# Query weights ahead of the first keys on the load queue, and one half of the key transpose further back, in a decode attention kernel

## The chip, the core and the metric

The kernel runs on one core of a Trainium2 chip. The metric is the device time of one execution in microseconds (us). Engines are called by short names: PE is the matrix engine (TensorE), PEld its weight loads, DVE the vector engine, ACT the scalar engine, POOL the GpSimd engine and SP the engine that issues most transfers. The 16 DMA engines bring data from the device memory (HBM) into the on-chip memory.

## What is computed

Eight sequences, one new token each. The token vectors (8 x 512) are normalized, an attention over the last 1024 cached positions gives s, a feed-forward network gives a gate g, and the output is x + s * g.

```python
xn = _layernorm(x)
q  = xn @ wq                            # 32 query heads of 128, 8 key/value heads
k  = k_cache[:, :, Sk - W:, :]          # W = 1024 of 4096 positions
v  = v_cache[:, :, Sk - W:, :]
p  = softmax(q . k * Dh ** -0.5)
s  = (p . v) @ wo                       # 4096 -> 512
g  = silu((gelu(xn @ w_gate) * (xn @ w_up)) @ w_down)
out = x + s * g
```

wq and wo have 4 MB each, the three feed-forward weights 1.75 MB each, and the windows of K and V 2 MB each for every one of the 8 batches. All of it is bf16 and is read once.

## The kernel before

**Loads.** The large arrays go through a pool of eight slots of 2 MB (`slot`, L62). `load_cache` (L70) loads K or V of one batch into a slot by two transfers of 1 MB, one for each group `g` of four heads; a partition receives one contiguous row of 8 KB. wq fills two slots, by two transfers of 2 MB with rows of 16 KB (L90 to L95). All of these are issued by SP, in the order of the program: `load_k(0)`, wq, `load_k(1)`, `load_v(0)`, and then, in the loop over batches (L399), `load_k(b + 2)` and `load_v(b + 1)`; behind the loop the feed-forward weights and wo (L420 to L438), the last quarter of wo in three pieces. A tile that needs a slot takes the one that has been out of use longest, and SP then also waits for the engine that read it last. A transfer also waits for the one that used the same completion semaphore before: there are eight of these, shared in turn by SP's transfers and the four small ones of x, which ACT issues (L68).

**Front.** DVE computes the statistics of x (L129) and the normalized x, PE transposes it, and DVE writes `xnR` (L153). Between them DVE, POOL and ACT prepare constants (L170 to L224). Then 32 matmuls (L248) multiply `xnR` with wq into eight accumulators, ACT and DVE cast them to bf16 (L258), DVE transposes them in 32 x 32 blocks (L261), and 16 copies by DVE and ACT (L270) place them in `qbd`, the block-diagonal query. `qbd` was set to zero before (L240).

**Batches.** K comes with positions on the partitions. `turn_k(b, g)` (L233) transposes one half of K of a batch on DVE, in 32 x 32 blocks of pairs, into one of three buffers `kT`. `scores(b, g)` (L281) multiplies with `qbd` on PE, eight matmuls for each half. `softmax(b)` (L304) takes the maximum on DVE and the exponential on ACT, `turn_p` (L327) transposes the probabilities on DVE, and `values(b)` (L334) multiplies with V on PE. `gather` and `regroup` (L355, L373) collect heads after batches 4 and 7. The schedule is written out by hand: each engine does its instructions in the order of the program. Before the loop, DVE has

```python
    turn_k(0, 0)
    turn_k(0, 1)
    nc.vector.memset(qbd, 0.0)
```

and then the casts, transposes and copies for q. In the loop the order for batch b is `turn_k(b+1, 0)`, `softmax(b)`, `scores(b+1, 0)`, `turn_k(b+1, 1)`, `scores(b+1, 1)`, `turn_p(b)`, `values(b)`.

**End.** The feed-forward network (L444 to L492) and the product with wo (L496 to L505, 32 matmuls for each of four quarters of wo) follow, then the gate and the residual (L507, L509) and the store (L511).

Of the kernel before, what the change touches and what calls it, by code (L numbers as in the profile page):

```python
# [21 lines left out]
def kernel(  # L22
# [13 lines left out]
    nc = tc.nc  # L36
# [25 lines left out]
    def slot(name):  # L62
        return ring.tile([P, 2 * ROW], BF16, name=name, tag="slot")
# [6 lines left out]
    def load_cache(cache, b, name):  # L70
        t = slot(name).rearrange("p (g x) -> p g x", g=NG)
        for g in range(NG):
            nc.sync.dma_start(  # L73
                out=t[:, g],
                in_=cache[b, g * HG : (g + 1) * HG, win0:Sk, :].rearrange(
                    "n (p c) d -> p n (c d)", c=C
                ),
            )
        return t
# [3 lines left out]
    def load_k(b):  # L83
        k_sb[b] = load_cache(A_k_cache, b, "k_sb")

    def load_v(b):
        v_sb[b] = load_cache(A_v_cache, b, "v_sb")

    load_k(0)
    wq_v = A_wq.rearrange("(p k) n -> p k n", k=NK)  # L90
    wq_sb = []
    for i in range(2):
        t = slot("wq_sb").rearrange("p (k n) -> p k n", k=NK // 2)
        nc.sync.dma_start(out=t, in_=wq_v[:, i * (NK // 2) : (i + 1) * (NK // 2), :])  # L94
        wq_sb += [t[:, k, :] for k in range(NK // 2)]  # L95
    load_k(1)
    load_v(0)

# [130 lines left out]
    qbd = keep.tile([P, 2, B, 2, NG, 4 * Hq], BF16, name="qbd")  # L229
# [3 lines left out]
    def turn_k(b, g):  # L233
        t = kT_pool.tile([P, ROW], BF16, name="kT")
        nc.vector.transpose(out=t.bitcast(I32), in_=k_sb[b][:, g].bitcast(I32))  # L235
        kT[b, g] = t

    turn_k(0, 0)
    turn_k(0, 1)
    nc.vector.memset(qbd, 0.0)  # L240
    q_both = slot("q_both")
    q_bf = q_both[:, 0:ROW]
    q_t = q_both[:, ROW : 2 * ROW]
# [20 lines left out]
    for j in range(4):  # L264
        sl = slice(32 * j, 32 * j + 32)
        for m in range(2):
            for g in range(NG):
                e = nc.scalar.copy if (4 * j + 2 * m + g) % 3 == 2 else nc.vector.tensor_copy
                c0 = j * Hq + g * qd
                e(out=qbd[sl, m, :, :, g, c0 : c0 + qd], in_=q_v[sl, m, :, 0, :, g, :])  # L270


    pT, S, P_sb, O_ps = {}, {}, {}, {}
# [270 lines left out]
```

## Time and profile before

| what | value |
|---|---|
| median of 3 runs | 121.66 us (121.61 to 121.68) |
| the profiled execution's own time | 121.48 us |
| its span in the profile | 119.4 us |
| busy in the span: DVE, PE, ACT, POOL | 75.8, 73.0, 31.4, 3.2 us |
| read from HBM | 47.46 MB, 397 GB/s over the span |
| K and V transfers: issue to landing, median | 19.7 and 20.0 us |

The span is the time between the first and the last record of the profiled execution; 2.1 us lie around it. A line of a timeline gives the start and the busy time in us, the engine, the line of the kernel, the operation, what it writes and reads, and in brackets how long the engine had been idle before it and what ended that wait. In the row of 40 slices each digit is the busy share in tenths, so a slice is 2.985 us.

### The profile page before, as it was taken

Reading aid. Unit: us, or ns where it says so; the run is one execution under the profiler, and the core shown is the slowest. Engines: PE = TensorE matmul, PEld = TensorE weight load, DVE = VectorE, ACT = ScalarE, POOL = GpSimd, SP = SyncE. Lnnn points to the kernel's source line nnn. Section 1 sums busy time; section 2 is a strip of 40 time slices with the busy share of each in tenths; the row PEclk is TensorE's granted clock in tenths of the full one; section 3 lists DMA queues with packets and bytes.
Section 4 is the critical chain, followed back from the end, with each engine's and each line's share of the span. In section 5 each row is a group of like instructions: output and inputs, shape, how many; then the busy total and the mean of one; then the engine's idle time right before and its main releaser. Section 6 shows DMA issues by size and latency. Waiting matters only on the chain.

```text
span 119.4 us, 2300 instructions
## 1 busy us (share of the span) xinstructions
PE 73.0 (61%) x985; PEld 38.7 (32%) x992; DVE 75.8 (63%) x101; ACT 31.4 (26%) x75; POOL 3.2 (3%) x10
## 2 busy tenths in 40 slices
PE   0001499811994987969687674991994547545370
PEld 0000134300341544535443351450453433143350
DVE  1048978399739999999959959909943241651000
ACT  2233000676007052341712510700616211200000
POOL 2006100000000000000000000000000000000000
PEclk9999999985599999999999998599589855555555
DMA  1999999999999999999999999999999999999930
GB/s 47 411 445 417 434 425 431 417 428 434 428 420 425 431 423 423 428 423 431 417 431 420 431 423 423 428 428 423 420 434 439 437 433 418 427 421 417 412 148 3
DMA packets 6254, 47.61 MB, mean 399 GB/s; under 512 B 732, under 2 KB 868, under 8 KB 1124
## 3 DMA queue, kind: packets, MB, share of 16 engines
q1 hardware_dynamic: 6228, 47.46, 94.3%
q8 instruction: 8, 0.13, 0.4%
q10 hardware_dynamic: 16, 0.01, 0.0%
q14 instruction: 2, 0.02, 0.0%
HBM read 47.46 MB, written 0.01 MB: 397 GB/s over the span
## 4 chain that ended last, share of the span: by engine, by line
DMA 85%; DVE 6%; PE 4%; SPq 2%; issue 1%
DMA k_sb<-in_A_k_cache_dram 48%; DMA wo_sb<-in_A_wo_dram 20%; DMA v_sb<-in_A_v_cache_dram 17%; DVE kT L235 4%; PE S_ps L296 2%; PE s_ps L499 1%; SPq L73 1%; DVE mx L306 1%; SPq L94 1%; PE O_ps L340 1%; PE r_ps L389 1%; DVE y L507 0%; DVE out_sb L509 0%; DVE oT L392 0%; DVE m L311 0%
## 5 line engine op out<-in xcount | busy, mean ns | idle before, releaser
L296 PE MATMUL S_ps<-kT,qbd 128*128 128x512 bf16 x128 | 34.1, 413 | 15.5 <-DVE kT L235 11.9
L235 DVE STREAM_TRANSPOSE kT<-k_sb 128x2048 int32<-128x2048 int32 x16 | 36.5, 2289 | 4.4 <-DMA k_sb<-in_A_k_cache_dram 4.3
L296 PEld LDWEIGHTS <-qbd 128*128 128x128 bf16 x128 | 12.8, 102 | 31.9 <-issue 16.4
L248 PE MATMUL q_ps<-wq_sb,xnR 128*128 128x512 bf16 x32 | 9.8, 481 | 4.3 <-DMA wq_sb<-in_A_wq_dram 4.3
L316 ACT ACTIVATE nb<-m 32x1 f32<-32x1 f32 x32 | 6.4, 201 | 22.5 <-DVE m L313 22.2
L306 DVE TENSOR_REDUCE mx<-S_ps 128x1 f32<-128x1024 f32 x8 | 9.6, 1196 | 4.1 <-PE S_ps L296 4.1
L318 ACT ACTIVATE P_sb<-S_ps,nb 128x1024 bf16<-128x1024 f32 x8 | 11.1, 1390 | 0.3
L340 PE MATMUL O_ps<-v_sb,pT 128*32 128x128 bf16 x512 | 9.1, 226 | 2.6 <-DVE pT L329 2.6
L340 PEld LDWEIGHTS <-pT 128*32 128x32 bf16 x512 | 7.6, 100 | 5.6 <-issue 3.0
L353 ACT COPY O_sb<-O_ps 128x256 f32<-128x256 f32 x8 | 3.0, 372 | 23.3 <-PE O_ps L340 23.3
L329 DVE STREAM_TRANSPOSE pT<-P_sb 128x512 int32<-128x512 int32 x8 | 5.7, 711 | 3.4 <-ACT P_sb L318 3.3
L248 PEld LDWEIGHTS <-xnR 128*128 128x128 bf16 x32 | 3.7, 118 | 10.1 <-issue 8.1
L361 PE MATMUL o_ps<-O_sb,sel 128*32 128x128 f32 x32 | 6.3, 332 | 0.9 <-ACT O_sb L353 0.9
L499 PE MATMUL s_ps<-wo_sb,oT 128*32 128x128 bf16 x128 | 4.4, 307 | 3.7 <-DMA wo_sb<-in_A_wo_dram 3.7
L258 ACT CAST q_both<-q_ps 128x512 bf16<-128x512 f32 x6 | 3.0, 611 | 12.2 <-PE q_ps L248 12.2
L151 PE MATMUL xnT_ps<-ident,xhat 8*128 8x8 bf16 x4 | 0.3, 174 | 8.9 <-DVE xhat L136 8.9
L499 PEld LDWEIGHTS <-oT 128*32 128x32 bf16 x128 | 3.5, 136 | 4.7 <-issue 4.5
L361 PEld LDWEIGHTS o_ps<-O_sb,sel 128*32 128x32 f32 x32 | 3.4, 128 | 5.0 <-issue 1.7
L507 DVE TENSOR_TENSOR y<-s_ps,g_sb 128x128 f32<-128x128 f32 x1 | 0.3, 292 | 7.2 <-PE s_ps L499 7.2
L285 PE MATMUL S_ps<-neg_mv,neg_st 128*128 128x512 bf16 x9 | 3.3, 384 | 1.9 <-DVE q_both L258 1.9
L129 DVE BATCH_NORM_STATS2 stats<-x_sb 8x6 f32<-8x512 bf16 x1 | 0.7, 681 | 5.7 <-DMA x_sb<-in_A_x_dram 5.7
L240 DVE MEMSET qbd<- 128x4096 uint32 x1 | 3.5, 3472 | 0.8 <-issue 0.8
(64 smaller groups left out, 51.2 us busy)
## 6 DMA issues: line engine op xcount, KB each, us to landing
k_sb<-in_A_k_cache_dram SPq DMA_DIRECT2D x16, 1024.0 KB, 19.7
v_sb<-in_A_v_cache_dram SPq DMA_DIRECT2D x16, 1024.0 KB, 20.0
wq_sb<-in_A_wq_dram SPq DMA_DIRECT2D x2, 2048.0 KB, 11.4
wo_sb<-in_A_wo_dram SPq DMA_DIRECT2D x3, 1024.0 KB, 25.1
wgu_sb<-in_B_w_gate_dram SPq DMA_DIRECT2D x1, 1792.0 KB, 21.4
wgu_sb<-in_B_w_up_dram SPq DMA_DIRECT2D x1, 1792.0 KB
wd_sb<-in_B_w_down_dram SPq DMA_DIRECT2D x1, 1792.0 KB
wo_sb<-in_A_wo_dram SPq DMA_DIRECT2D x1, 640.0 KB
```

The source lines that it names most:

```text
L235: nc.vector.transpose(out=t.bitcast(I32), in_=k_sb[b][:, g].bitcast(I32))
L240: nc.vector.memset(qbd, 0.0)
L248: nc.tensor.matmul(q_ps[i], xnR[:, k, :, :].rearrange("p j b -> p (j b)"), wq_sb[k][:, i * 512 : (i + 1) * 512], start=(k == 0), stop=(k = ...
L285: nc.tensor.matmul(S[b][:, half, :], neg_st.rearrange("p j h -> p (j h)"), neg_mv.rearrange("p a n -> p (a n)"), start=True, stop=False,)
L296: nc.tensor.matmul(S[b][:, half, :], qbd[:, m, b, w, g, :], kv[:, half * 16 : (half + 1) * 16, m, :, w], start=False, stop=(g == NG - 1 an ...
L306: nc.vector.tensor_reduce(out=mx, in_=S[b].rearrange("p a c -> p (a c)"), axis=AX.X, op=ALU.max)
L316: nc.scalar.mul(nb[32 * j : 32 * j + 32, :], m1, -inv)
L318: nc.scalar.activation(out=P_sb[b].rearrange("p c i w -> p c w i"), in_=S[b].rearrange("p a (c w i) -> p (a c) w i", w=2, i=32), func=ACT.Exp,
L329: nc.vector.transpose(out=pT[b].rearrange("p c h w -> p (c h w)").bitcast(I32), in_=P_sb[b].rearrange("p c i w -> p (c i w)").bitcast(I32),)
L340: nc.tensor.matmul(O_ps[b][32 * t : 32 * t + 32, g, :], pT[b][:, c // 2, :, c % 2], vv[:, c, :], start=(c < 4), stop=(c >= C - 4),)
L361: nc.tensor.matmul(o[:, 0:Dh], sel[:, g, :], O_sb[b][:, g, :], start=(g == 0), stop=(g == NG - 1))
L499: nc.tensor.matmul(s_ps[32 * t : 32 * t + 32, :], oT[:, j, u, :], wo[u][:, j, t * DT : (t + 1) * DT], start=(u == 0 and j == 0), stop=(u = ...
```

## The change

wq is issued ahead of both halves of K of batch 0. On DVE, `qbd` is set to zero ahead of the first `turn_k`, and `turn_k(0, 1)` stands behind the copies into `qbd`. No instruction is added or taken out.

```diff
-    load_k(0)
     wq_v = A_wq.rearrange("(p k) n -> p k n", k=NK)
     wq_sb = []
     for i in range(2):
         t = slot("wq_sb").rearrange("p (k n) -> p k n", k=NK // 2)
         nc.sync.dma_start(out=t, in_=wq_v[:, i * (NK // 2) : (i + 1) * (NK // 2), :])
         wq_sb += [t[:, k, :] for k in range(NK // 2)]
+    load_k(0)
     load_k(1)
     load_v(0)
...
-    turn_k(0, 0)
-    turn_k(0, 1)
     nc.vector.memset(qbd, 0.0)
+    turn_k(0, 0)
     q_both = slot("q_both")
...
                 e(out=qbd[sl, m, :, :, g, c0 : c0 + qd], in_=q_v[sl, m, :, 0, :, g, :])
+    turn_k(0, 1)
```

More of the change, by code (lines that the diff above doesn't have):

```diff
@@ L236, in turn_k @@
         kT[b, g] = t
+    nc.vector.memset(qbd, 0.0)
     turn_k(0, 0)
-    turn_k(0, 1)
-    nc.vector.memset(qbd, 0.0)
     q_both = slot("q_both")
```

## The prediction

> **What bounds the kernel now.** I read the table of 40 slices and the chain of waits on the page first, then the busy time by stage, then the timelines of DVE, PE and SP's queue.
>
> ```profile
> DMA  1999999999999999999999999999999999999930
> GB/s 47 411 445 417 434 425 431 417 428 434 428 420 425 431 423 423 428 423 431 417 431 420 431 423 423 428 428 423 420 434 439 437 433 418 427 421 417 412 148 3
> ...
> DMA 85%; DVE 6%; PE 4%; SPq 2%; issue 1%
> ```
>
> See that the 16 DMA engines are full in every slice from the second to the third from the end, and that 85% of the chain is transfer time. The next view is busy time by stage (stage, its length, four engines and POOL, granted clock, DMA share, GB/s).
>
> ```profile
> 2.50:10.00 7.50, 0.51 (x8) 0.31 (x8) 2.16 (x10) 3.08 (x5) 0.06 (x1) 1.00 1.01 418
> 10.00:17.50 7.50, 3.79 (x9) 1.31 (x10) 6.53 (x10) 0.00 (x0) 2.33 (x3) 1.00 1.00 429
> ...
> 17.50:32.50 15.00, 9.71 (x34) 3.66 (x33) 12.24 (x19) 5.86 (x11) 0.00 (x0) 0.79 1.01 425
> 40.00:74.00 34.00, 26.19 (x436) 14.74 (x440) 30.39 (x29) 10.82 (x29) 0.00 (x0) 1.00 1.01 425
> 112.00:117.00 5.00, 2.30 (x64) 1.68 (x63) 0.58 (x2) 0.00 (x0) 0.00 (x0) 0.50 0.53 208
> ```
>
> The rate is the same with K rows (8 KB), wq rows (16 KB) or V rows on the way. So 47.46 MB from 2.5 us on at about 425 GB/s need 112 us and end near 114.2 us; the last transfers land at 114.8 us and a little after. Does compute hold that stream up? The DVE and PE timelines answer:
>
> ```profile
> 7.02 0.68 DVE L129 BATCH_NORM_STATS2 stats<-x_sb 8x6 f32<-8x512 bf16 x1 [5.71 <-DMA x_sb<-in_A_x_dram]
> ```
>
> ```profile
> 13.71 9.80 PE L248 MATMUL q_ps<-wq_sb,xnR 128*128 128x512 bf16 x32 [4.29 <-DMA wq_sb<-in_A_wq_dram]
> ```
>
> ```profile
> 34.78 1.23 DVE L306 TENSOR_REDUCE mx<-S_ps 128x1 f32<-128x1024 f32 x1 [2.62 <-PE S_ps L296]
> ```
>
> ```profile
> 61.08 2.31 DVE L235 STREAM_TRANSPOSE kT<-k_sb 128x2048 int32<-128x2048 int32 x1 [1.34 <-DMA k_sb<-in_A_k_cache_dram]
> ...
> 80.81 2.31 DVE L235 STREAM_TRANSPOSE kT<-k_sb 128x2048 int32<-128x2048 int32 x1 [3.00 <-DMA k_sb<-in_A_k_cache_dram]
> ```
>
> ```profile
> 108.38 1.04 PE L499 MATMUL s_ps<-wo_sb,oT 128*32 128x128 bf16 x32 [0.41 <-DMA wo_sb<-in_A_wo_dram]
> ...
> 110.86 1.04 PE L499 MATMUL s_ps<-wo_sb,oT 128*32 128x128 bf16 x32 [1.44 <-DMA wo_sb<-in_A_wo_dram]
> ...
> 113.31 1.04 PE L499 MATMUL s_ps<-wo_sb,oT 128*32 128x128 bf16 x32 [1.40 <-DMA wo_sb<-in_A_wo_dram]
> ...
> 114.84 1.25 PE L499 MATMUL s_ps<-wo_sb,oT 128*32 128x128 bf16 x32 [0.49 <-DMA wo_sb<-in_A_wo_dram]
> ```
>
> The first softmax waits for scores at 34.78, late: K of batch 0 came long before. Its successors follow every 6.76 us (34.78, 41.58, 48.34, 55.10 in the DVE timeline), while K plus V of a batch (4.19 MB) need 9.9 us of transfer. So compute gains about 3.1 us a batch, and at 61.08 DVE waits for K: the front's delay is gone. At 80.81 it waits 3.00 us, and each quarter of wo is waited for (0.41 + 1.44 + 1.40 + 0.49 = 3.74 us). SP's queue, in the view of its waits up to 62 us, waited for nothing but landings (19.7 us K, 15.5 us V, 8.5 us wq): the next issue waits for an older transfer, with about 20 us from issue to landing, so some 8 MB stand in the queue.
>
> **The change, part by part.** No instruction is added or removed; bytes and sizes stay.
>
> *Two wq transfers pass two K transfers on SP's queue.* By cumulated bytes: the second wq half completes 4.19 MB, which landed at 13.6 us before (the first half then; the SP issue that waited for it is at 13.59). The first half, 2.1 MB, should land at 8.7 us (2.5 + 4.9, plus 1.2 us of landing lag, read from 13.6 against 2.5 + 4.19/0.425). K's two halves follow at 16.0 and 18.4 us (the second wq half released an issue at 18.42). Everything behind keeps its place.
>
> What SP waits for shifts too. Before, the sixth SP transfer (K of batch 1, second half) waited until 6.22 us, the first K half's landing; the same semaphore then belongs to the first wq half, 8.7 us. By then 5.2 MB are still queued (wq second half, K0, one piece of K1), 12.3 us of work. The second half of K2 will wait for the second wq half, 13.6 us, with 7.3 MB queued, 17 us. V1's first half goes at 16.0 instead of 13.59; all after that as now. The stream doesn't run dry: cost 0. If this cover were gone, each us of lateness beyond 12 us would cost a us.
>
> *Slots.* The pool gives slots in order of last use. K3 now takes the first wq slot (PE), V2 the second, K4 that of q_both (DVE, ACT), V3 that of K0 (second turn), K5 that of K1 as before. Issue times to meet: 20.95, 25.82, 30.75, 36.02 us.
>
> *x.* The four x transfers go by ACT's queue and landed at 7.0 us, 4.5 us after data began, behind 1.9 MB of K. Now they stand beside wq. Lower end: they wait as many bytes, 7.0. Upper end: they wait as many rows, twice as long each, up to all of wq: 2.5 + 4.2/0.425 = 12.4 us. I take the upper end, since the row shows x held behind nearly both K pieces; the lower stays in the working.
>
> The Trainium skill speaks against the change here: "DMA: Bandwidth & Descriptors", section "Queues, rings and completion order", says that an engine alternates between queues only after a whole packet of some 9 to 17 descriptors. By that page x would pay for wider rows and land near 12 us, by equal bytes at 7; the trace shows 7.0 behind narrow rows and cannot settle it, and the sum is the same by both.
>
> *The front chain, early case (x at 7.0).* xnR is ready at 9.75 (7.02 + 2.73), q matmuls run 9.8 to 19.6 (9.80 us as now; the 17th starts at 16.6 at the earliest, with wq landed at 13.6), 3.9 us earlier. DVE ends its small work at 11.76, sets qbd to zero until 15.2 (3.47 us), waits for K until 16.0 and turns until 18.3; the first DVE cast is due at 22.75 − 3.9 = 18.8. Casts, transposes and copies then take what they took: scores start at 29.40 − 3.9 = 25.5. The moved turn (2.3 us) stands behind DVE's copies, 25.9 to 28.2; PE meanwhile does the first eight score matmuls at the 0.43 us spacing that the first matmuls show now (granted clock 0.61 from 25 to 30 us), 3.4 us, until 28.9: hidden, else it costs up to 2.3 us there. First maximum near 30.9.
>
> *Late case (x at 12.4).* xnR at 15.1, q matmuls to 24.9, 1.4 us later than now; memset and first turn end at 22.9, before the cast at 24.1; scores at 30.8; moved turn 31.2 to 33.5 under PE's work until 34.2; first maximum near 36.2. SP's K3 waits for the first 16 q matmuls until some 21.5, 0.6 us late, with 16 us in the queue.
>
> So the front shifts by −3.9 to +1.4 us. What is late next? Compute reaches the transfers' pace one or two batches sooner (K4 lands near 50.7 us) or at about the same place; then it waits for K. Before it costs anything, lateness must eat 1.34 + 3.00 + 3.74 = 8.1 us of waits. At 50.7 the first turn of K4, before at 52.91, simply waits longer. PE idles more in those batches; with such idling the clock was 0.76 to 0.84 instead of 1.00, but the batch from 70.9 to 80.8, with clock 0.50 in part of it, still left 3.00 us.
>
> Sum: 121.48 us of the profiled execution (119.4 span + 2.1 around it) + 0 = 121.48. That execution is 0.18 us below the median of the runs, 121.66, to which the change will be compared; I forecast **121.6**.
>
> **Rivals.**
>
> *Uneven start and finish, faster.* The first 7.5 us move 418 GB/s, the next 429: 0.19 us short. In the last 5 us 1.04 MB go at 208 GB/s; at 425 they would take 2.45 us and end at 114.45, against the landing at 114.80: 0.35 us from engines that do not finish together. Wide rows first might smooth either; both together give −0.54, so 121.1. For: the two rows. Against: the order at the end is unchanged.
>
> *The same, slower.* Place: the last 3 us, where the slowest of 16 engines decides. One row more on that engine is 16 KB at 425/16 = 26.6 GB/s, 0.62 us (8 KB: 0.31). If its arrears grow by one wide row, 122.3; by a narrow one, 122.0. It decides from 0.24 us, so one row. Against: equal shares per transfer.
>
> *The front was on the path.* Then the 3.9 us would come off: 117.7. Against: the waits for K at 61.08 and 80.81.
>
> *Compute falls behind.* Lateness over 8.1 us would cost what exceeds it; 10 us would give 123.6. The latest working above is +1.4.
>
> *It doesn't do what it says:* x late takes the early start away (late case). Still 121.6.
>
> **How the numbers follow.** No change 0.70 (121.6, in either case of x); uneven, faster 0.13; front on the path 0.03; uneven, slower 0.11; behind 0.03. A measurement of this kernel can tell about 0.2%, 0.24 us. Hence faster 0.16, same 0.70, slower 0.14. The range takes in the forecast's own 121.4 to 121.9 and most of both uneven cases: 121.2 to 122.1.
>
> **What would show it.** Right: the DMA row full throughout; q matmuls near 9.8 or 15; qbd copies ending near 26 or 31; DVE waiting for K from about 51 or 61 us on; wo's last quarter near 114.8. Wrong: a slice short of 9 on the DMA row behind an SP wait on PE or DVE; no DVE wait for K at 80 us; the last landing moved by more than 0.3 us, which would mean that the stream's rate or its finish depends on order.

## The result and the profile after

The changed kernel takes 121.25 us (median of 13 runs, 120.84 to 121.45), the kernel before beside it 121.53 us (13 runs, 121.14 to 121.72). The ratio is 0.9973 with a 95% interval of 0.9961 to 0.9985, so it is faster by 0.27%, about 0.33 us. A second comparison gave 0.9973 again (0.9960 to 0.9987). The forecast was 121.6 us in a range of 121.2 to 122.1, with no change beyond 0.2% as the likeliest case at 0.70 and faster at 0.16. The gain is small but it is there, and the forecast's sum had nothing for it: what came is the case given 0.16. That the time still lies in the range is luck, since the range was drawn down to 121.2 for a rival with another cause.

The page of the changed kernel, its row of slices and its chain of waits:

```profile
DMA  4999999999999999999999999999999999999930
GB/s 94 429 425 440 407 418 426 431 431 420 420 440 420 420 429 431 412 429 434 420 418 429 437 415 420 437 423 423 423 434 429 452 414 433 422 408 434 402 137 3
...
DMA 59%; PE 16%; DVE 15%; ACT 3%; issue 2%; ACTq 1%; DVEq 0%
```

The stream is full in the same slices, but the first slice has 4 instead of 1 and 94 GB/s instead of 47: the data begin earlier. The chain now runs through PE and DVE in the front. That looks as if compute had become the bound; experiment 3 shows that it has not.

Busy time by stage, before (stage, its length, PE, PEld, DVE, ACT, POOL, granted clock, DMA share, GB/s):

```profile
0.00:1.60 1.60, 0.00 (x0) 0.00 (x0) 0.38 (x3) 0.00 (x0) 0.67 (x7) 1.00 0.00 0
1.60:2.40 0.80, 0.00 (x0) 0.00 (x0) 0.00 (x0) 0.03 (x1) 0.12 (x1) 1.00 0.03 3
2.40:3.20 0.80, 0.00 (x0) 0.00 (x0) 0.00 (x0) 0.80 (x1) 0.00 (x0) 1.00 0.92 328
...
0.00:5.50 5.50, 0.00 (x0) 0.00 (x0) 0.38 (x3) 1.28 (x1) 0.79 (x7) 1.00 0.53 208
5.50:110.00 104.50, 69.67 (x889) 36.12 (x897) 74.84 (x96) 30.09 (x74) 2.38 (x3) 0.86 1.01 427
```

The same stages, after:

```profile
0.00:1.60 1.60, 0.00 (x0) 0.00 (x0) 0.39 (x3) 0.00 (x0) 0.67 (x7) 1.00 0.00 0
1.60:2.40 0.80, 0.00 (x0) 0.00 (x0) 0.00 (x0) 0.13 (x1) 0.11 (x1) 1.00 1.37 289
2.40:3.20 0.80, 0.00 (x0) 0.00 (x0) 0.00 (x0) 0.80 (x1) 0.00 (x0) 1.00 0.68 246
...
0.00:5.50 5.50, 0.00 (x0) 0.00 (x0) 0.39 (x3) 1.28 (x1) 0.78 (x7) 1.00 0.67 239
5.50:110.00 104.50, 70.83 (x896) 36.13 (x897) 74.83 (x96) 30.13 (x74) 2.38 (x3) 0.85 1.01 426
```

Between 1.6 and 2.4 us the kernel before moves nothing but x (3 GB/s); the changed one already moves wq. Over the first 5.5 us it moves 239 GB/s against 208, and from there on the two are equal, 426 and 427 GB/s. (A row of data counts in full where it starts, so the rate of a short stage with 16 KB rows is too high; a DMA share over 1 shows that.)

DVE and PE in the changed kernel, in order of time (start, busy, engine, line, operation, wait and releaser):

```profile
8.68 0.68 DVE L129 BATCH_NORM_STATS2 stats<-x_sb 8x6 f32<-8x512 bf16 x1 [7.37 <-DMA x_sb<-in_A_x_dram]
...
32.72 1.23 DVE L306 TENSOR_REDUCE mx<-S_ps 128x1 f32<-128x1024 f32 x1 [1.36 <-PE S_ps L296]
...
51.21 2.31 DVE L235 STREAM_TRANSPOSE kT<-k_sb 128x2048 int32<-128x2048 int32 x1 [0.29 <-DMA k_sb<-in_A_k_cache_dram]
...
60.79 2.31 DVE L235 STREAM_TRANSPOSE kT<-k_sb 128x2048 int32<-128x2048 int32 x1 [2.70 <-DMA k_sb<-in_A_k_cache_dram]
```

```profile
11.60 8.61 PE L247 MATMUL q_ps<-wq_sb,xnR 128*128 128x512 bf16 x32 [0.52 <-ACT x_res L163]
...
113.15 1.04 PE L499 MATMUL s_ps<-wo_sb,oT 128*32 128x128 bf16 x32 [1.46 <-DMA wo_sb<-in_A_wo_dram]
...
114.69 1.22 PE L499 MATMUL s_ps<-wo_sb,oT 128*32 128x128 bf16 x32 [0.50 <-DMA wo_sb<-in_A_wo_dram]
```

The first maximum comes 2.06 us earlier (32.72 against 34.78). Of that nothing is left at 60.79: DVE only waits longer for K there, 2.70 us instead of 1.34. What remains is that K itself comes 0.29 us earlier, and the last quarter of wo 0.15 us earlier in this execution.

### The profile page after: what moved, and what is told of

Read it like the earlier page. It is cut to its first block, busy times and chain, and to the rows that moved or that the text cites. A ratio compares the mean times of both kernels' runs of the same rounds, so it can differ in the third digit from the quotient of the medians.

```text
span 119.2 us, 2307 instructions
## 1 busy us (share of the span) xinstructions
PE 74.1 (62%) x992; PEld 38.7 (32%) x992; DVE 75.8 (64%) x101; ACT 31.4 (26%) x75; POOL 3.2 (3%) x10
## 4 chain that ended last, share of the span: by engine, by line
DMA 59%; PE 16%; DVE 15%; ACT 3%; issue 2%; ACTq 1%; DVEq 0%
DMA wo_sb<-in_A_wo_dram 20%; DMA k_sb<-in_A_k_cache_dram 17%; DMA v_sb<-in_A_v_cache_dram 17%; PE S_ps L296 7%; PE q_ps L247 7%; DVE kT L235 6%; DMA x_sb<-in_A_x_dram 6%; DVE mx L306 3%; DVE qbd L269 2%; DVE q_both L260 1%; ACT P_sb L318 1%; ACT L146 1%; PE s_ps L499 1%; DVE q_both L257 1%; ACTq L68 1%
## 5 line engine op out<-in xcount | busy, mean ns | idle before, releaser
L296 PE MATMUL S_ps<-kT,qbd 128*128 128x512 bf16 x128 | 35.8, 429 | 16.2 <-DVE kT L235 12.8
L247 PE MATMUL q_ps<-wq_sb,xnR 128*128 128x512 bf16 x32 | 8.6, 437 | 0.5 <-ACT x_res L163 0.5
L361 PE MATMUL o_ps<-O_sb,sel 128*32 128x128 f32 x32 | 5.6, 304 | 0.9 <-ACT O_sb L353 0.9
L285 PE MATMUL S_ps<-neg_mv,neg_st 128*128 128x512 bf16 x16 | 4.8, 382 | 2.2 <-DVE q_both L257 2.2
```

The costliest lines, as they stand in the source:

```text
L247: nc.tensor.matmul(q_ps[i], xnR[:, k, :, :].rearrange("p j b -> p (j b)"), wq_sb[k][:, i * 512 : (i + 1) * 512], start=(k == 0), stop=(k = ...
L285: nc.tensor.matmul(S[b][:, half, :], neg_st.rearrange("p j h -> p (j h)"), neg_mv.rearrange("p a n -> p (a n)"), start=True, stop=False,)
L296: nc.tensor.matmul(S[b][:, half, :], qbd[:, m, b, w, g, :], kv[:, half * 16 : (half + 1) * 16, m, :, w], start=False, stop=(g == NG - 1 an ...
L361: nc.tensor.matmul(o[:, 0:Dh], sel[:, g, :], O_sb[b][:, g, :], start=(g == 0), stop=(g == NG - 1))
```

## The experiments

Three theories stood at the start. **S**: the stream of transfers begins earlier because another transfer is the first one. **C**: the q chain comes earlier, and that is worth something. **U**: the 16 DMA engines finish less unevenly, by a chance of the order. All ratios are against the kernel before, run beside each on the same chip.

### 1. The loads alone

```diff
-    load_k(0)
     wq_v = A_wq.rearrange("(p k) n -> p k n", k=NK)
...
+    load_k(0)
     load_k(1)
```

> Only the loads are moved (wq ahead of K of batch 0); DVE's order is that of before. Theory S (the stream of transfers starts earlier because a wq transfer is the first one): all of the gain, 0.2 to 0.45 us faster than before, first large data near 1.8 us instead of 2.5, and about 0.12 MB more moved by 5.5 us. Theory C (the q chain comes earlier and that is on the path): less than half of the gain, since the second turn of K0 stands ahead of the casts again and waits for K until about 18 us. Theory U (engines finish less unevenly by chance of order): no fixed relation to the start.

Measured: 121.24 us against 121.58, ratio 0.9970 (0.9957 to 0.9984). The loads alone give the whole gain. The first maximum is at 36.16 us here, 1.4 us later than before, so theory C falls already.

### 2. DVE's order alone

```diff
-    turn_k(0, 0)
-    turn_k(0, 1)
     nc.vector.memset(qbd, 0.0)
+    turn_k(0, 0)
...
+    turn_k(0, 1)
```

> Only DVE's order is changed (memset first, second turn of K0 behind the copies); K0 is loaded ahead of wq as before. Theory S: same as before within 0.15 us, first large data near 2.5 us. Theory C: the scores start at the same time as before (q matmuls still wait for wq until 13.7 us), so no gain or a loss of up to 2 us at the front; if the front were on the path a loss would show at the end.

Measured: 121.58 us against 121.58, ratio 1.0000 (0.9991 to 1.0009). The first maximum comes at 33.89 us instead of 34.78, and that is worth nothing. It is not shown that DVE's order brought this: 0.66 us of the 0.89 is already there at the first cast of q on DVE (22.09 against 22.75), since the q matmuls began 0.22 us earlier in this execution and took 9.36 us instead of 9.80.

### 3. Stream early, compute late

```diff
-    for i in range(2):
+    for i in (1, 0):
         t = slot("wq_sb").rearrange("p (k n) -> p k n", k=NK // 2)
         nc.sync.dma_start(out=t, in_=wq_v[:, i * (NK // 2) : (i + 1) * (NK // 2), :])
...
-    load_k(0)
...
+        if i == 1:
+            load_k(0)
```

> The second half of wq goes first, then K0, then the first half of wq; DVE's order as in the changed kernel. The q matmuls begin with the half that comes last, near 18.4 us, so the first softmax is about 5 us later than before. Theory S: the first transfer is still a wq transfer, so 0.2 to 0.45 us faster than before, although compute is later than in either kernel. Theory C: slower than before, by up to 5 us.

Measured: 121.32 us against 121.58, ratio 0.9972 (0.9960 to 0.9983). DVE in this kernel:

```profile
38.69 1.23 DVE L308 TENSOR_REDUCE mx<-S_ps 128x1 f32<-128x1024 f32 x1 [0.27 <-PE S_ps L298]
...
80.67 2.31 DVE L237 STREAM_TRANSPOSE kT<-k_sb 128x2048 int32<-128x2048 int32 x1 [0.43 <-DMA k_sb<-in_A_k_cache_dram]
```

and what SP's queue waited for (total us, times, longest):

```profile
SPq L73 <- PE q_ps L249: 5.9, 2, 3.7
SPq L73 <- DVE qbd L271: 5.1, 1, 5.1
```

The first maximum is 3.91 us later than before, SP held loads back for compute, once for 5.1 us, and the kernel is still faster than before by as much as the changed one. The lateness is paid out of the waits: 1.34 + 3.00 - 3.91 = 0.43, and 0.43 is left at 80.67. (That it fits to the hundredth is chance: K comes 0.14 us earlier here, and DVE is ready for it 2.43 us later than before, not 3.91 - 1.34 = 2.57.) Whatever the chain of waits of the changed kernel runs through, the front is not on the path. Theory S stands, C is refuted.

### 4. Is it the width of the rows?

```diff
-        nc.sync.dma_start(out=t, in_=wq_v[:, i * (NK // 2) : (i + 1) * (NK // 2), :])
+        if i == 0:
+            for k in range(NK // 2):
+                nc.sync.dma_start(out=t[:, k, :], in_=wq_v[:, k, :])
...
```

> As the changed kernel, but the first half of wq comes by two transfers of 1 MB with rows of 8 KB instead of one of 2 MB with rows of 16 KB. Theory S with the cause in how a wq transfer is issued (128 plain rows, 0.39 us to issue against 0.66 for K's four-head form): first data again near 1.8 us; the first rows then take some 0.5 us instead of over 1.1, so the lead grows: 0.3 to 0.7 us faster than before. Theory S with the cause in the width of the rows: first data near 2.5 us and no gain.

Measured: 121.36 us against 121.58, ratio 0.9976 (0.9963 to 0.9989). 187 GB/s already flow from 1.6 to 2.4 us and 247 over the first 5.5 us, so rows of 8 KB start as early as rows of 16 KB: the width is not the cause. The larger gain that was expected did not come.

### 5. K first, head by head

```diff
-    load_k(0)
+    for n in range(HG):
+        nc.sync.dma_start(
+            out=t0[32 * n : 32 * n + 32, 0],
+            in_=A_k_cache[0, n, win0:Sk, :].rearrange("(p c) d -> p (c d)", c=C),
+        )
...
```

> The kernel before, with K of batch 0 still first, but its first half loaded by four transfers, one per head, each of 32 plain rows of 8 KB (256 KB). Form theory (a transfer of plain rows is issued and started sooner than K's form over four heads): first large data near 1.8 us although K comes first, and 0.15 to 0.45 us faster than before. Array theory (it matters that wq and not K is read first): first data near 2.3 to 2.5 us and the same time as before within 0.15 us.

Each head now fills 32 neighbouring partitions, where the kernel before interleaves the four heads, so part of the computation is on other data.

Measured: 123.08 us against 121.53, ratio 1.0126 (1.0102 to 1.0151), slower. The start is as the form theory has it, though K comes first:

```profile
1.60:2.40 0.80, 0.00 (x0) 0.00 (x0) 0.00 (x0) 0.15 (x1) 0.12 (x1) 1.00 0.88 207
2.40:3.20 0.80, 0.00 (x0) 0.00 (x0) 0.00 (x0) 0.80 (x1) 0.00 (x0) 1.00 1.17 320
3.20:5.50 2.30, 0.00 (x0) 0.00 (x0) 0.00 (x0) 0.33 (x1) 0.00 (x0) 1.00 0.97 212
```

But then the full engines (share 0.97) move only 212 GB/s, and the last quarter of wo comes at 116.41 instead of 114.84. The edit brought a second cost that hid the first effect, so by its time this run decides nothing. It led to experiment 7.

### 6. V first

```diff
-    load_k(0)
+    load_v(0)
     wq_v = A_wq.rearrange("(p k) n -> p k n", k=NK)
...
+    load_k(0)
     load_k(1)
-    load_v(0)
```

> V of batch 0 first (same four-head form as K, another array), then wq, K of batch 0, K of batch 1; DVE's order as before. Form theory: first data at 2.3 to 2.5 us as with K first, and the same time as before within 0.15 us, with compute later. Array theory, that K in particular starts late: first data near 1.8 us and 0.2 to 0.4 us faster.

Measured: 121.51 us against 121.53, ratio 1.0002 (0.9985 to 1.0019). V has K's form over four heads; its issue takes 0.67 us, 115 GB/s flow from 1.6 to 2.4 us, and nothing is gained. Experiment 2, with K first, has 105 GB/s there and nothing gained either; over the first 5.5 us the two move 208 and 214 GB/s, the kernel before 208. This run also answers theory C once more: its first maximum is at 41.95 us, 7.17 us later than before, and nothing is lost either.

### 7. K first, in plain rows

```diff
-    load_k(0)
+    nc.sync.dma_start(
+        out=t0[:, 0],
+        in_=A_k_cache[0, 0, :, :].rearrange("(p c) d -> p (c d)", c=C),
+    )
...
```

> The kernel before, K first, but the first half of K of batch 0 is one transfer of 128 plain rows of 8 KB that are contiguous in memory (all 4096 positions of head 0), instead of the windows of four heads: as many bytes and rows, all partitions, but the wrong positions of K for that half, so part of the computation is on other data. Form theory: issued in about 0.40 us instead of 0.66, first large data near 1.8 us, 240 to 250 GB/s over the first 5.5 us, and 0.15 to 0.45 us faster than before, with no transfer moved. If K as an array or its place ahead of wq matters, first data near 2.3 to 2.5 us and no gain.

Measured: 121.19 us against 121.58, ratio 0.9967 (0.9954 to 0.9980). No transfer is moved and DVE's order is that of before. How SP issues the first transfer, here and then in the kernel before (start, duration in us):

```profile
0.81 0.39 SPq L90 DMA_DIRECT2D k_sb<-in_A_k_cache_dram  x1
```

```profile
0.80 0.66 SPq L73 DMA_DIRECT2D k_sb<-in_A_k_cache_dram  x1
```

The issue takes 0.39 us, as for wq in the changed kernel. When data begin shows in stages of 0.2 us: first here, then in experiment 2, which loads in the order of the kernel before, then in the kernel before:

```profile
1.80:2.00 0.20, 0.00 (x0) 0.00 (x0) 0.00 (x0) 0.00 (x0) 0.00 (x0) 1.00 1.82 328
...
0.00:5.50 5.50, 0.00 (x0) 0.00 (x0) 0.39 (x3) 1.28 (x1) 0.79 (x7) 1.00 0.61 227
```

```profile
2.20:2.40 0.20, 0.00 (x0) 0.00 (x0) 0.00 (x0) 0.02 (x1) 0.00 (x0) 1.00 2.31 410
...
0.00:5.50 5.50, 0.00 (x0) 0.00 (x0) 0.38 (x3) 1.28 (x1) 0.79 (x7) 1.00 0.60 214
```

```profile
2.20:2.40 0.20, 0.00 (x0) 0.00 (x0) 0.00 (x0) 0.03 (x1) 0.00 (x0) 1.00 0.00 0
2.40:2.60 0.20, 0.00 (x0) 0.00 (x0) 0.00 (x0) 0.20 (x1) 0.00 (x0) 1.00 1.32 328
```

The rate from 1.6 to 2.4 us alone would decide nothing: it is 125 GB/s here, 105 and 115 in experiments 2 and 6 without a gain, and 3 in the kernel before. But data begin between 1.8 and 2.0 us here and in every other execution with a plain transfer first (the two of the changed kernel, the two with narrow rows, experiments 1, 3 and 5), and between 2.2 and 2.6 us in the three with a four-head transfer first. The 227 GB/s over the first 5.5 us are more than the 208 and 214 with the four-head form, but fewer than the 240 to 250 expected. The run gives the whole gain, so the cause is the form of the transfer that goes first, and neither wq nor the order behind it. That the rows also lie elsewhere in memory here is no way out for the start: experiment 5 reads the windows of before in plain rows and begins as early.

### 8. The changed kernel again, and the narrow rows beside it

> The changed kernel once more, beside the next one on one chip: 0.2 to 0.45 us faster than before by the theory of the earlier stream; no difference from before if the first comparison was chance.

> The changed kernel with the first wq half in rows of 8 KB once more, beside the changed kernel. If its larger lead at 5.5 us (247 GB/s over the first 5.5 us against 239) reaches the end, it is 0.1 to 0.2 us faster than the changed kernel; if the finish takes it back, the two are the same.

Measured on one chip: the changed kernel 121.25 us, ratio 0.9973 (0.9960 to 0.9987); with the narrow rows of experiment 4 121.37 us, ratio 0.9988 (0.9974 to 1.0002), both against 121.53. The narrow rows do not beat the changed kernel. In their two profiled executions the last quarter of wo is at 114.39 and 114.48 us, and at 114.69 and 114.54 in the two of the changed kernel; why their timed runs show none of that is open.

## Why the prediction was right and wrong, point by point

**The bound: right.** The stream sets the end, at 427 and 426 GB/s from 5.5 us on, and compute waits for it. Experiments 3 and 6 spend 3.91 and 7.17 us of the 8.1 us of waits without a loss; the whole of it was not tried.

**"The stream doesn't run dry: cost 0": right.** SP's issues fell later than before by up to 3.2 us in experiment 3 (24.16 against 20.95) and by up to 4.9 us in experiment 6 (45.79 against 40.87), without a loss.

**The landings: all about half a microsecond too late, and here is the step that failed.** "The first half, 2.1 MB, should land at 8.7 us (2.5 + 4.9, plus 1.2 us of landing lag)" took the 2.5 us at which data began from the kernel before, as if every first transfer began there. The issues that wait for those landings now stand at 8.15 (8.7 predicted) for the first wq half, and at 15.44 and 17.93 (16.0 and 18.4) for K's two halves. The sum's "+ 0" left out this term, which measured about 0.33 us. The rows of before had only a weak hint: 0.66 us to issue the first K transfer, and 0.63 and 0.47 us for the two of wq (L94). I counted which transfers pass which, but not that the very first one is issued with nothing to hide it. The faster rival named the start as well, but guessed at smoother rows (0.19 us) and at an unchanged beginning.

**x: the end that I took was the wrong one.** DVE's first work on x is at 8.68 us, between 7.0 and 12.4 and nearer the lower end. The Trainium skill, "DMA: Bandwidth & Descriptors", section "Queues, rings and completion order", with its whole packets of some 9 to 17 descriptors per turn, would have put x near 12 us by the estimate in the prediction; the measured 8.68 us speaks against that estimate. It does not speak against the page: at 26.6 GB/s, the prediction's rate of one engine, some 11 rows of 16 KB pass between 1.9 and 8.68 us (an estimate), and x comes just behind the first wq transfer (8.15, by the issue that waits for it), as it came just behind the first K transfer before (6.22, x at 7.02). Where a packet ends, no run shows. It changes nothing at the end.

**The front: right within its ends.** The first q matmul came at 11.60 (9.8 to 15.1 predicted), the first maximum at 32.72 (30.9 to 36.2), and the moved turn was hidden: the sixteen score matmuls run from 26.40 without a wait. DVE first waits for K at 51.21, predicted near 51.

**The rivals.** Uneven finish, in either direction, is not needed: wherever a plain transfer of 128 rows went first the ratio was 0.9967 to 0.9988 (the interval of the last one alone reaches 1.0002), and with the four-head form first it was 1.0000 and 1.0002. The front on the path, 117.7 us, is refuted by experiments 1, 3 and 6.

What stays open is why a first transfer over four heads puts its data off. Its issue is 0.27 us longer, but data begin 0.2 to 0.8 us later by the stages of 0.2 us. The sizes do not follow each other either: by the bytes moved in the first 5.5 us, at 427 GB/s, the lead over the kernel before is 0.25 us in experiment 7, 0.40 in the changed kernel and 0.50 in experiment 4 (estimates, each from one execution), while by the ratios they are faster by 0.40, 0.33 and 0.29 us, with intervals that overlap. So the direction is shown, and how much of a lead reaches the end is not.

## What to carry to other kernels

Where transfers keep the DMA engines full to the end and compute has waits to spare, as here, reordering compute is worth nothing, and the time can only change where the stream begins, where it ends, or in its rate; so look first at the transfer that starts it. Put a transfer there that is quick to issue, of plain rows over all partitions. And test "is this on the path?" by making the thing later on purpose, as experiments 3 and 6 do: that decides what a chain of waits leaves open.

## What the hardware showed that was not expected

- 1 MB from K's array took 0.66 us to issue as windows of four heads and 0.39 us as 128 plain rows, both as the first transfer of SP (experiment 7 and the kernel before); the median of all four-head transfers of the kernel before was 0.535 us. The form alone does not set the time of an issue: wq's plain transfers took 0.39 and 0.41 us as the first two in the changed kernel, and 0.63 and 0.47 us as the third and fourth before.
- Four transfers of 32 rows each instead of one of 128 came with half the rate, 212 GB/s from 3.2 to 5.5 us with the engines 97% busy, and with 1.26% more time in all (experiment 5). Each such transfer writes to a quarter of the partitions; that this is the cause is argued, not shown.
- A chain of waits went from 85% to 59% DMA between two kernels with the same bound: it follows the last releaser, even where some 8 MB were still queued behind it (an estimate: 20 us from issue to landing at 425 GB/s).
